# Five units of the first batch alone, the second batch behind the weights, and float32 turns on TensorE

## The chip, the cores and the metric

The kernel runs on one core of a Trainium2 chip, in one launch. The metric is the device time of a run in microseconds; the kernel before takes 768.63 us (median of 3 runs, 768.42 to 770.69).

Names of engines: PE is TensorE (matmuls and transposes), PEld its weight loads, DVE is VectorE, ACT is ScalarE, POOL is GpSimd, SP is SyncE, whose queue issues nearly all transfers between HBM (the device memory) and SBUF (the on-chip memory). PSUM is the memory that PE writes to.

## The reference

Block-sparse attention followed by a feed-forward layer, cut to what matters:

```python
# q, k, v: 4 batches x 8 heads x 768 positions x 64, float32; blocks of 32 positions (24 blocks)
scores = q @ k.T / sqrt(64)            # masked: a block sees itself and its two neighbours,
                                       # blocks 0 and 23, and 3 sampled blocks; blocks 0 and 23 see all
attn = exp(scores - max); attn /= attn.sum(-1, keepdims=True) + 1e-9
x = (attn @ v).transpose(0, 2, 1, 3).reshape(3072, 512)
h = x @ w_in                           # 512 x 2048, float64 in HBM
g = np.where(h > 0, h, exp(min(h, 0)) - 1)
out = g @ w_out                        # 2048 x 512, float64 in HBM; out is float32
```

## The kernel before

The 3072 rows are worked off in 24 units of 128 rows (four query blocks of 32). The four batches are taken as two pairs; batch 0 of a pair is x=0 and batch 1 is x=1. A unit of `of_one` (L608) takes four neighbouring blocks of one batch, a unit of `of_two` (L605) two blocks of both batches, and the special unit blocks 0 and 23 of both. `ALONE` (L303) says how many units of the first pair are of one batch: 1, so unit 0 is of x=0, unit 1 of x=1, and all later ones need both batches.

**Precision.** A float32 value is carried as two float16 parts, a high and a low one (the high part is a cast, the low one the value less the high part), and products are taken over the parts. Queries and keys are split and turned (transposed), values are split with a column of ones beside them.

**Attention of a unit** (`attention`, L656), by pairs of heads (four pairs hp=0..3): PE makes the scores (L786, 32 matmuls of 32 columns for one pair: against `kG`, where POOL has gathered the sampled blocks' keys, L748 and L755, and against the neighbours in `kT`); DVE takes the maxima (L797); ACT the exponentials `e` (L815); then `e` is cast to the high part of `p` (L818) and the low part taken from it (L820, DVE or POOL); `p` (eight squares of 128) is turned by `turn16` (L374), either on PE into PSUM with a copy out by ACT or DVE (L391), or by a transfer on SP's queue (L377); PE multiplies with the values (L835, 64 matmuls); DVE adds the two parts (L844). After four pairs DVE normalizes (L852 to L854), `x` is split (L863, L864) and turned into `xT` (L866). The values lie in HBM as `vd`, written by the kernel in float16 with the ends of the sequence doubled (L569), and a unit's rows are fetched into the rooms `VT` by SP (L726 to L728) and by an indirect transfer on POOL (L733).

**Feed-forward** (`ffn`, L870), for two units at once (U=0..11), in 8 steps f2 of two chunks of 128 of the 2048 hidden values: layer 1 (L883, 24 matmuls into `h`), the activation on ACT and DVE (L893, L895, L891), its split into `g` (L898, L900), layer 2 (L906, 12 matmuls into the two `o`).

**Weights.** 32 pieces of 512 KB, float64. Each is loaded as pairs of integers into a room that waits to be filled (`wo_room`, the place of later output weights, or `st4`), and made into float16 parts by six operations (`weights`, L417): ACT scales the upper words (L439), ACT or DVE shifts (L444, L448), DVE takes signs (L451) and joins (L455), ACT or DVE casts the high part (L459), DVE or POOL takes the low part (L462). A step f2 of the feed-forward needs four pieces.

**What sets the order.** All operations are given to a planner (`Plan`, L43) with a priority, the engines that may take them with a cost each, what they read and write, and the buffer they need (`rooms`, L260, says how many there are of each tag). `Plan.order` (L70) places them in one list, engine by engine, and the engines then work off their lists in that order, waiting on semaphores. So the numbers at the end (L921 to L951) decide what stands ahead of what on each engine, SP's queue included. There: the keys and values of x=0 at -500, those of x=1 at `SECOND` = -110, the weights from `WI` = -100 on, `WID` = 3 apart, the feed-forward U at `F0 + T * U` with steps `F2` = 4.5 apart, attention `LEAD` = 130 ahead of it. Units below `NPE` = 4 have all their turns on PE; units 4 to 13 have the first two pairs (`PP` = 2) turned on PE and the rest by transfers.

Lines touched: `turn16` (L374), `weights` with its rooms (L401 to L472), `zero_rows` (L480), `keys` and `values` (L576, L586), the copy into `kG` (L738 to L757), `e32`, `p` and `pT` (L810 to L823), `norm` and the split of `x` (L850 to L867), `ffn` (L870) and the numbers (L303, L921 to L951).

## Time and profile before

| | |
|---|---|
| device time, median of 3 runs | 768.63 us |
| profiled execution (its span; nothing outside the span is recorded) | 780.8 us |
| PE busy | 703.2 us, 90% of the span |
| DVE, ACT, POOL busy | 504.7, 406.1, 398.8 us |
| bytes moved by transfers | 126.34 MB, 162 GB/s over the span |

The profile is of one execution, 12.2 us (1.6%) longer than the median of the timed runs; durations come from it. Busy time says that an engine had an instruction under way. The granted clock tells how fast PE ran: 1.0 is 2.4 GHz and 0.5 is 1.2 GHz. Lines (L883) are those of the listing above.

### The profile page before, as it was taken

Reading aid. Unit: us, or ns where it says so; the run is one execution under the profiler, and the core shown is the slowest. Engines: PE = TensorE matmul, PEld = TensorE weight load, DVE = VectorE, ACT = ScalarE, POOL = GpSimd, SP = SyncE. Lnnn points to the kernel's source line nnn. Section 1 sums busy time; section 2 is a strip of 40 time slices with the busy share of each in tenths; the row PEclk is TensorE's granted clock in tenths of the full one; section 3 lists DMA queues with packets and bytes.
Section 4 is the critical chain, followed back from the end, with each engine's and each line's share of the span. In section 5 each row is a group of like instructions: output and inputs, shape, how many; then the busy total and the mean of one; then the engine's idle time right before and its main releaser. Section 6 shows DMA issues by size and latency. Waiting matters only on the chain.

```text
span 780.8 us, 26302 instructions
## 1 busy us (share of the span) xinstructions
PE 703.2 (90%) x11064; PEld 476.2 (61%) x11064; DVE 504.7 (65%) x849; ACT 406.1 (52%) x723; POOL 398.8 (51%) x605
## 2 busy tenths in 40 slices
PE   6445466999999998999999999999999999999997
PEld 3334355666665765666866766657656667676663
DVE  7788778898866772767677665757555546644121
ACT  4597767897753743535575443425414344342221
POOL 2588567677553345554375454645625337443121
PEclk7555569999999999999999999999999999999999
DMA  9899998889749697769947987987349459652101
GB/s 240 263 275 288 261 257 209 215 158 208 154 91 264 187 192 164 161 133 203 221 87 142 171 149 150 183 144 166 76 94 229 69 103 216 141 97 45 38 1 27
DMA packets 217006, 126.34 MB, mean 162 GB/s; under 512 B 173944, under 2 KB 194552, under 8 KB 216888
## 3 DMA queue, kind: packets, MB, share of 16 engines
q1 hardware_dynamic: 211608, 107.09, 64.8%
q0 software_dynamic: 5280, 17.58, 8.9%
q8 instruction: 86, 1.41, 0.8%
q14 instruction: 32, 0.26, 0.1%
HBM read 82.05 MB, written 13.21 MB: 122 GB/s over the span
## 4 chain that ended last, share of the span: by engine, by line
PE 80%; issue 4%; DMA 4%; DVE 4%; ACT 3%; POOL 3%; POOLq 1%; SPq 1%; another core or an unknown queue 1%; ACTq 0%; DVEq 0%
PE o L906 32%; PE h L883 31%; PE s L786 6%; PE w L835 4%; PE av L835 2%; PE s L385 2%; DMA wo<-in_moe_w_out_dram 2%; ACT e L815 1%; PE av L385 1%; POOLq L751 1%; DMA VT<-vd 1%; POOL kG L755 1%; DMA raw<-in_sampled_blocks_dram 1%; POOL kG L748 1%
## 5 line engine op out<-in xcount | busy, mean ns | idle before, releaser
L883 PE MATMUL h<-xT,wi 128*128 128x256 f16 x2304 | 281.6, 275 | 4.7 <-DVE fe L891 4.0
L906 PE MATMUL o<-wo,g 128*128 128x512 f16 x1152 | 274.9, 381 | 0.9 <-issue 0.6
L883 PEld LDWEIGHTS <-wi 128*128 128x128 f16 x2304 | 220.0, 98 | 53.8 <-issue 7.1
L906 PEld LDWEIGHTS <-g 128*128 128x128 f16 x1152 | 107.0, 98 | 111.2 <-issue 4.2
L900 POOL TENSOR_TENSOR g<-fe,g 128x512 f16<-128x512 f32 x75 | 90.0, 1200 | 150.8 <-DVE g L299 134.8
L820 POOL TENSOR_TENSOR p<-e,p 128x512 f16<-128x512 f32 x94 | 113.1, 1206 | 93.8 <-DVE p L299 46.4
L893 ACT ACTIVATE fe<-h 128x512 f32<-128x512 f32 x96 | 57.3, 596 | 178.0 <-PE h L883 165.1
L891 DVE SCALAR_TENSOR_TENSOR fe<-h,fe 128x512 f32<-128x512 f32 x96 | 66.0, 688 | 92.9 <-ACT fe L895 84.4
L815 ACT ACTIVATE e<-s,m 128x256 f32<-128x256 f32 x208 | 86.2, 470 | 74.7 <-POOL p L820 37.1
L755 POOL COPY kG<-kT 128x128 int32 x264 | 78.5, 341 | 44.9 <-PE s L786 25.9
L797 DVE TENSOR_REDUCE m<-s 128x2 f32<-128x512 f32 x104 | 70.1, 686 | 44.4 <-PE s L786 41.4
L733 POOL DMA_INDIRECT VT<-vd,idx x66 | 64.5, 977 | 25.1 <-issue 10.1
L895 ACT ACTIVATE fe<-fe,gs 128x512 f32<-128x512 f32 x96 | 69.4, 723 | 2.4
L844 DVE TENSOR_REDUCE x<-w 128x130 f32<-128x260 f32 x64 | 27.2, 426 | 59.7 <-PE w L835 56.9
L835 PEld LDWEIGHTS <-pT 128*32 128x32 f16 x3456 | 43.2, 97 | 36.1 <-issue 33.7
L786 PE MATMUL s<-kG,qT 128*32 128x160 f16 x704 | 44.8, 247 | 9.6 <-ACT e L815 7.0
L786 PEld LDWEIGHTS <-qT 128*32 128x32 f16 x1664 | 33.2, 99 | 31.8 <-issue 26.7
L786 PE MATMUL s<-kT,qT 128*32 128x96 f16 (+1 forms) x832 | 48.5, 225 | 1.2 <-issue 1.0
L786 PE MATMUL s<-kT,qS 128*32 128x96 f16 (+1 forms) x832 | 48.3, 225 | 0.5 <-issue 0.5
L786 PE MATMUL s<-kG,qS 128*32 128x160 f16 x704 | 44.2, 246 | 4.1 <-DVE qS L299 2.7
L299 DVE CAST p<-e 128x512 f16<-128x512 f32 x59 | 32.0, 546 | 13.3 <-DMA pT<-p 6.1
L786 PEld LDWEIGHTS <-qS 128*32 128x32 f16 x1664 | 34.5, 102 | 6.0 <-DVE qS L299 3.0
(134 smaller groups left out, 812.5 us busy)
## 6 DMA issues: line engine op xcount, KB each, us to landing
VT<-vd SPq DMA_DIRECT2D x44, 195.0 KB
VT<-vd SPq DMA_DIRECT2D x22, 390.0 KB
wo<-in_moe_w_out_dram SPq DMA_DIRECT2D x12, 512.0 KB
st<-in_q_dram SPq DMA_DIRECT2D x40, 128.0 KB
out_dram<-ro SPq DMA_DIRECT2D x38, 128.0 KB
wo<-in_moe_w_in_dram SPq DMA_DIRECT2D x9, 512.0 KB
st<-in_moe_w_in_dram SPq DMA_DIRECT2D x7, 512.0 KB
VT<-vd SPq DMA_DIRECT2D x12, 260.0 KB
```

What stands on the lines that cost most here:

```text
L733: nc.gpsimd.indirect_dma_start(VT[0:96, 2 * vt.slot, xs[0] : xs[-1] + 1].rearrange("p b x -> p (b x)"), None, d.ap, bass.IndirectOffsetOnA ...
L755: nc.gpsimd.tensor_copy(dst[:, :, r * 16 : (r + 1) * 16], src[:, :, bass.ds(at[r], 16)])
L786: nc.tensor.matmul(dst, lhsT=qq.ap[:, h, j * BLK : (j + 1) * BLK], rhs=mv, start=first, stop=(y == 1 and qq is qS and o0 + w == 256))
L797: nc.vector.tensor_reduce(m.ap[:, 2 * c : 2 * c + 2] if sp else m.ap[:, 6:8], ss[c].ap, axis=AX.X, op=ALU.max, negate=True)
L815: nc.scalar.activation(e32.ap[:, y, :], ss[c].ap[:, y, :], AF.Exp, bias=m.ap[:, 6 + y : 7 + y])
L820: plan.add(LO, t + PITCH * hp + 1, margin=MO, fn=lambda e, e32=e32, p=p: ENG[e].tensor_tensor(p.ap[:, 1, :], flat(e32.ap), p.ap[:, 0, :], ...
L835: nc.tensor.matmul(av.ap[j * BLK : (j + 1) * BLK, y, v0:], lhsT=pts[c].ap[:, pl * 4 + y * 2 + z, j * BLK : (j + 1) * BLK], rhs=VT[:, room, ...
L883: nc.tensor.matmul(h.ap[:, a, :], lhsT=w[:, wl, cs], rhs=x.ap[:, xl, cc, :], start=(n == 0), stop=(n == 3 * NCC - 1))
L891: nc.vector.scalar_tensor_tensor(e32.ap, h.ap, -IH * GS, e32.ap, op0=ALU.mult, op1=ALU.min)
L895: plan.add({"ACT": 0.68}, p0 + 2.6, lambda e, e32=e32: nc.scalar.activation(e32.ap, e32.ap, AF.Relu, bias=gs_col, scale=-GS), r=[e32], w=[ ...
L900: plan.add(LO, p0 + 2.6, margin=MO, fn=lambda e, e32=e32, g=g: ENG[e].tensor_tensor(g.ap[:, 1], e32.ap, g.ap[:, 0], op=ALU.subtract), r=[e ...
L906: nc.tensor.matmul(o.ap, lhsT=g.ap[:, gl, f % 2, m * P : (m + 1) * P], rhs=wo[f][:, wl, :], start=(f == 0 and n == 0), stop=(f == NFC - 1 ...
```

## The change

The first pair's first five units are now of x=0 alone (`ALONE` = 5), then five of x=1, then the special unit and one of both batches; before, all but two needed both. Only the keys and values of x=0 are loaded ahead of the weights, values first. Those of x=1 follow at `SECOND` = 28, behind most of the weights, by the functions `keys` and `values` that the second pair has used so far. Until then the room of x=1's keys, `kT1`, is lent to the weights as three more landing rooms. Feed-forward 0 stands at -50 with steps 12 apart, feed-forward 1 at 60.

A new function `turn32` turns float32 squares on PE (four of 128 x 128 in place of eight in float16) into PSUM; ACT casts the high part out of PSUM, and DVE takes the low part as PSUM less the high part. It replaces the cast, the low part and the `turn16` of `p` and `x` where these went by PE: all pairs and `x` of units 0 to 5 (`NPE` = 6, was 4), the first two pairs of units 6 to 13 without the special one. From unit 6 on, `e` and `p` of the odd pairs lie together in one `st4` buffer (not close to the change of pairs).

The diff, cut:

```diff
+class Part:
+    def __init__(self, whole, view):
+        self.whole, self.view = whole, view
+    @property
+    def ap(self):
+        return self.view()
...
-    ALONE, SPECIAL, SECOND = 1, 8, -110.0
-    MO, MC, ML, MH = -0.6, 0.0, 0.5, 0.6
+    ALONE, SPECIAL, SECOND, KT_LAST, ST_FIRST = 5, 10, 28.0, 32, 20
+    MO, MC, ML, MH, MW = -0.6, 0.0, 0.5, 0.6, 0.0
...
+    def turn32(t, src, part, high, low, new=(), w=(), name="", bank="s"):
+        pt = buf(bank, [P, 4, P], F32, ps)
+        def go(e):
+            for i in range(4):
+                nc.tensor.transpose(pt.ap[:, i, :], part(i), ident)
+        plan.add({"PE": TURN32}, t, go, r=[src], new=[pt], code=8, name=name + "p")
+        plan.add(HIGH, t, lambda e: scaled(e, high(), pt.ap), r=[pt], new=new, w=w, margin=MC, port=False, name=name)
+        plan.add({"DVE": 0.69}, t, lambda e: nc.vector.tensor_tensor(low(), pt.ap, high(), op=ALU.subtract),
+                 r=[pt, *new, *w], w=[*new, *w], port=False, name=name + "l")
+
+    TURN32, HIGH = 0.6, {"ACT": 0.6}
...
-    used = {j: j - 20 for j in range(NFC // 2)}
+    kt_room = [fixed(flat(kT[1])[:, 2048 * j : 2048 * (j + 1)].bitcast(I32).rearrange("p (e w) -> p e w", w=2))
+               for j in range(3)]
+    ROOMS = {**{j: wo_room[j] for j in range(NFC // 2)}, **{-3 - j: r for j, r in enumerate(kt_room)}}
+    used = {j: j - 20 for j in ROOMS}
...
-        free_rooms = [j for j in used if j > n // 4]
-        if n // 4 >= 4:
+        free_rooms = [j for j in used if j > n // 4 or j < -2 and n < KT_LAST]
+        if n >= ST_FIRST:
...
-        plan.add({"SP": 0.5}, prio, load, new=[s] * tagged, w=[s] * (not tagged), dma=1.9, name=f"wl{i}")
+        plan.add({"SP": 0.5}, EARLY_AT if n < EARLY else prio, load, new=[s] * tagged, w=[s] * (not tagged), dma=1.9, name=f"wl{i}")
...
-        plan.add(SHIFT, prio, lower, margin=MH, r=[s], new=[low3], name=f"ws{i}")
+        plan.add(SHIFT, prio, lower, margin=MW, port=False, r=[s], new=[low3], name=f"ws{i}")
...
-        plan.add({"ACT": 0.6, "DVE": 0.43}, prio, high, margin=MH, r=[s], w=[hi_done, *over], name=f"wh{i}")
+        plan.add({"ACT": 0.6, "DVE": 0.43}, prio, high, margin=MW, r=[s], w=[hi_done, *over], name=f"wh{i}")
...
-    def keys(g, x, c, prio, via="DMA"):
+    def keys(g, x, c, prio, via="DMA", over=()):
...
-        turn16(prio, n, lambda: kT[x][:, :, c * P : (c + 1) * P], via, w=[kT_buf[x][c]],
+        turn16(prio, n, lambda: kT[x][:, :, c * P : (c + 1) * P], via, w=[kT_buf[x][c], *over],
...
-    def values(g, c, prio):
-        n = buf("st4", [P, 2, H, VW], F16)
+    def values(g, c, prio, xs=(0, 1)):
+        n = buf("st4", [P, len(xs), H, VW], F16)
...
-                e32, p, pT = buf("e", [P, 2, 256], F32), buf("p", [P, 2, 512], F16), buf("g" if u == 1 else "pT", [P, 8, P], F16)
+                pT = buf("g" if u == 1 else "pT", [P, 8, P], F16)
+                if u >= WIDE and hp % 2 and not sp and not NUP - OFF <= u < NUP + ON:
+                    both = buf("st4", [P, 2, 512], F32)
+                    e32 = Part(both, lambda both=both: both.ap[:, 0].rearrange("p (y k) -> p y k", y=2))
+                    p = Part(both, lambda both=both: both.ap[:, 1].bitcast(F16).rearrange("p (l k) -> p l k", l=2))
+                else:
+                    e32, p = buf("e", [P, 2, 256], F32), buf("p", [P, 2, 512], F16)
...
+                if hp < via[1] and not sp:
+                    turn32(t + PITCH * hp + TURN, eb, lambda i, e32=e32: flat(e32.ap)[:, i * P : (i + 1) * P],
+                           lambda pT=pT: pT.ap[:, 0:4], lambda pT=pT: pT.ap[:, 4:8], new=[pT], name=f"pt{u}.{hp}", bank=bank)
+                    continue
...
+        if via[2] == "PE":
+            turn32(t + PITCH * 3 + TIMES + 3, xf, lambda i: xf.ap[:, i * P : (i + 1) * P],
+                   lambda: xt.ap[:, 0, :, ts_], lambda: xt.ap[:, 1, :, ts_],
+                   new=new, w=[] if new else [xt], name=f"xt{u}", bank="av")
+            return
...
-    EVEN, NEXT = 6, 14.0
+    EVEN, NEXT = 6, 4.0
+    WIDE, OFF, ON = 6, 3, -1
...
-    TWO, AHEAD, T, F0, LEAD, NPE = 6, 16.0, 58.0, 60.0, 130.0, 4
-    WI, WID, F2, LAG = -100.0, 3.0, 4.5, 14.0
-    V1, K1 = 70.0, 16.0
+    TWO, AHEAD, T, F0, LEAD, NPE = 6, 16.0, 58.0, 60.0, 130.0, 6
+    WI, WID, F2, LAG = -66.0, 3.0, 4.5, 14.0
+    V1, K1, SV = 70.0, 16.0, 8.0
+    EARLY, EARLY_AT = 5, -95.0
...
-    for x in range(2):
-        p = -500 if x == 0 else SECOND
-        places = [wo_place(j) for j in range(6)] if x == 0 else [wi_place(j) for j in range(2, 8)]
...
+    F1, F2X = (-50.0, 60.0), 12.0
...
+            if u == 4 * ALONE // 4:
+                for c in range(NKC):
+                    keys(0, 1, c, SECOND + 2 * c, "PE", kt_room)
+                for c in range(NKC):
+                    values(0, c, SECOND + SV + 2 * c, (1,))
...
-        ffn(U, t)
+        ffn(U, F1[U] if U < len(F1) else t, F2X if U == 0 else F2)
```

How this moves instructions, at three places. **SP's queue where the weights begin**, before (L511 loads keys and values, `wi<-in_k_dram` being the keys of x=1; L569 writes values to `vd`; L429 loads a weight piece):

```order
L511 DMA wo<-in_v_dram 128x8x128 x3
L511 DMA wi<-in_k_dram 128x8x128 x3
L569 DMA vd_175<-st_171 16x1040 x2
L569 DMA vd_175<-st_171 7x16x1040 x2
L429 DMA wo<-in_moe_w_in_dram 128x4x256
L640 DMA st_428<-in_q_dram 128x8x64
```

and now the same queue at the last weight pieces (L457 and L461 load pieces, L605 keys and L618 values of x=1, `kT_71` is the room of x=1's keys):

```order
L457 DMA kT_71<-in_moe_w_in_dram 128x4x256
L605 DMA st_2644<-in_k_dram 128x8x64
L461 DMA kT_71<-in_moe_w_out_dram 128x1024
L605 DMA st_2657<-in_k_dram 128x8x64
L461 DMA kT_71<-in_moe_w_out_dram 128x1024
L605 DMA st_3109<-in_k_dram 128x8x64
L618 DMA st_3132<-in_v_dram 128x8x64
L605 DMA st_3151<-in_k_dram 128x8x64
```

The keys of x=1 stood ahead of all weights and now stand between and behind the last of them, the values behind all.

**PE where feed-forward 0 begins**, before (L786 are scores, of unit 3 here; `h<-xT,wi` is layer 1):

```order
L786 LDWEIGHTS qS_2075
L786 MATMUL s_2130<-kT_71,qS_2075 32x96
L786 LDWEIGHTS qS_2075
L786 MATMUL s_2130<-kT_71,qS_2075 32x96
L883 LDWEIGHTS wi
L883 MATMUL h_2164<-xT_1553,wi 128x256
```

and now (L880 multiplies unit 1's last pair with the values, L412 is a float32 turn, of unit 1's `x`):

```order
L880 MATMUL av_1542<-VT,g_1397 32x65
L880 LDWEIGHTS g_1397
L880 MATMUL av_1542<-VT,g_1397 32x65
L412 MATMUL av_1589<-ident,xn_1581 128x128 x4
L936 LDWEIGHTS wi
L936 MATMUL h_1607<-xT_1488,wi 128x256
```

Before, 416 score matmuls (three units and a quarter) and 12 turns of keys stood ahead of the first layer 1; now it comes as soon as unit 1 is turned, with 256 score matmuls and 6 turns of keys ahead.

**DVE over unit 0's pairs**, before (L797 maxima, L299 a cast, L451 and L455 weights):

```order
L797 TENSOR_REDUCE m_750<-s_713 128x2
L299 CAST p_790<-e_752 128x512
L797 TENSOR_REDUCE m_805<-s_757 128x2
L451 SCALAR_TENSOR_TENSOR w_792<-wo,w_792 128x512
L455 SCALAR_TENSOR_TENSOR wo<-wo,w_792 128x512
```

and now (L831 maxima, L415 the low part of a float32 turn, L528 the low part of a query, L479 and L483 weights):

```order
L831 TENSOR_REDUCE m_687<-s_641 128x2
L415 TENSOR_TENSOR pT_679<-o_632,pT_679 128x512
L528 SCALAR_TENSOR_TENSOR n_691<-st_431,n_691 128x8x64
L415 TENSOR_TENSOR pT_727<-o_674,pT_727 128x512
L831 TENSOR_REDUCE m_806<-s_693 128x2
L479 SCALAR_TENSOR_TENSOR w_638<-kT_71,w_638 128x512
```

Each turned pair has one low part on DVE, read from PSUM, where it had casts, low parts and copies shared out over three engines.

## Rows read from the trace of the kernel before

**Rows 1.** The page's 40 slices of 19.5 us: granted clock of PE in tenths.

```profile
PEclk7555569999999999999999999999999999999999
```

**Rows 2.** Six stretches: length, busy PE, PEld, DVE, ACT, POOL (instructions), clock, DMA, GB/s.

```profile
0.00:50.70 50.70, 26.48 (x327) 18.78 (x328) 37.63 (x73) 31.53 (x49) 25.26 (x69) 0.65 0.92 263
50.70:124.90 74.20, 43.98 (x964) 33.53 (x962) 60.53 (x91) 57.91 (x101) 52.01 (x80) 0.62 0.98 264
124.90:196.20 71.30, 63.20 (x1134) 43.62 (x1134) 61.44 (x97) 57.64 (x104) 51.00 (x84) 0.95 0.85 189
196.20:302.00 105.80, 103.64 (x1715) 68.67 (x1714) 76.01 (x130) 57.54 (x106) 47.38 (x63) 1.00 0.80 174
302.00:370.00 68.00, 62.13 (x1081) 42.16 (x1079) 42.73 (x76) 31.80 (x56) 36.63 (x43) 0.97 0.85 170
370.00:780.80 410.80, 403.76 (x5852) 269.42 (x5849) 226.40 (x386) 169.64 (x312) 186.49 (x270) 1.00 0.63 122
```

**Rows 3.** PE in order of time: start, length, line, operation, idle before.

```profile
34.79 0.33 PE L786 MATMUL s<-kG,qT 128*32 128x160 f16 x4
...
113.00 1.97 PE L883 MATMUL h<-xT,wi 128*128 128x256 f16 x12
```

**Rows 4.** The weights' last load and last low part: durations, then first and last start.

```profile
L433 SPq DMA_DIRECT2D st<-in_moe_w_out_dram x4: 346/360/364, 115.0 to 179.5; - x4
...
L462 POOL TENSOR_TENSOR wo<-st,wo x2: 1170/1296/1422, 185.1 to 195.1; 128x512 f16<-128x512 f32 x2
```

**Rows 5.** Groups of DVE, shapes apart: count, busy us, mean ns, idle before.

```profile
L797 DVE TENSOR_REDUCE m<-s 128x2 f32<-128x512 f32 x104 | 70.1, 686 | 44.4 <-PE s L786 41.4 <-remote 2.5
L891 DVE SCALAR_TENSOR_TENSOR fe<-h,fe 128x512 f32<-128x512 f32 x96 | 66.0, 688 | 92.9 <-ACT fe L895 84.4 <-POOL kG L755 3.1 <-ACT kT L297 1.8
...
L299 DVE CAST p<-e 128x512 f16<-128x512 f32 x59 | 32.0, 546 | 13.3 <-DMA pT<-p 6.1 <-ACT e L815 5.0 <-issue 1.0
L671 DVE COPY qS<-qT 64x1024 f16<-64x1024 f16 x40 | 30.8, 771 | 1.0
...
L820 DVE TENSOR_TENSOR p<-e,p 128x512 f16<-128x512 f32 x18 | 16.4, 911 | 0.2
...
L844 DVE TENSOR_REDUCE x<-av 128x130 f32<-128x260 f32 x32 | 13.5, 422 | 19.2 <-remote 10.9 <-PE av L835 7.7 <-PE s L385 0.6
...
L497 DVE SCALAR_TENSOR_TENSOR VT<-wi,VT 128x512 f16<-128x512 f32 x6 | 8.5, 1415 | 0.0
...
L497 DVE SCALAR_TENSOR_TENSOR fe<-wi,fe 128x512 f16<-128x512 f32 x6 | 4.3, 741 | 0.0
```

**Rows 6.** From 196.2 us on, one line each: L883, L906, L786, L835, L385 (busy, matmuls).

```profile
196.20:780.80 584.60, 247.65 (x2040) 1.00 0.69 137
196.20:780.80 584.60, 254.01 (x1068) 1.00 0.69 137
196.20:780.80 584.60, 51.69 (x2432) 1.00 0.69 137
196.20:780.80 584.60, 47.21 (x2848) 1.00 0.69 137
196.20:780.80 584.60, 19.27 (x256) 1.00 0.69 137
```

**Rows 7.** The chain that ended last: start, length, what.

```profile
299.20 0.56 PE s L786 x32
299.76 2.70 PE o L906 x12
302.46 1.31 PE h L883 x12
303.77 0.46 PE av L835 x32
```

**Rows 8.** PE in order of time: a float16 turn of eight squares, and what follows it.

```profile
310.81 0.61 PE L385 MATMUL av<-ident,p 128*128 128x128 f16 x8 [3.29 <-issue]
311.35 0.25 PE L786 MATMUL s<-kG,qT 128*32 128x160 f16 x4
```

More of the change, by code (lines that the diff above doesn't have):

```diff
@@ L315 @@
     kG = const([P, rooms["kG"], 2, H, KW], F16, "kG")
-    ident = sb.tile([P, P], F32, tag="x32", bufs=rooms["x32"], name="ident")
+    ident = const([P, P], F32, "ident")
     nc.gpsimd.memset(ident, 1.0)
@@ L377, in turn16 @@
             plan.add({"SP": 1.3}, t, lambda e: nc.sync.dma_start_transpose(dst(), flat(src.ap)),
-                     r=[src], new=new, w=w, dma=2.4, name=name)
+                     r=[getattr(src, "whole", src)], new=new, w=w, dma=2.4, name=name)
             return
+        got = getattr(src, "whole", src)
         pt = buf(bank, [P, 8, P], F16, ps)
@@ L420, in weights @@
         w = (wi if i < NFC else wo)[f]
[L421 removed]
+        s = ROOMS[stage[n]] if stage[n] in ROOMS else buf("st4", [P, DM, 2], I32)
         over = [wo_room[f // 2]] if i >= NFC else []
@@ L478, with zero_rows, put @@
     vd += [[(buf("vd1", [ROWS, 2 * RW], F16, dr), (0, 1))] for _ in range(1, NPAIR)]
-    def zero_rows(prio):
-        z = buf("st4", [P, 2 * RW], F16)
+    def zero_rows(prio, later):
+        z = buf("x32", [P, RW], F16)
         plan.add({"POOL": 0.6}, prio, lambda e: nc.gpsimd.memset(z.ap[0:BLK, :], 0.0), new=[z], name="zero")
         for g in range(NPAIR):
-            for n in (0, NB - 1):
-                for d, xs in vd[g]:
-                    def put(e, d=d, xs=xs, n=n):
-                        nc.sync.dma_start(d.ap[n * BLK : (n + 1) * BLK, :], z.ap[0:BLK, 0 : RW * len(xs)])
-                    plan.add({"SP": 0.45}, prio, put, r=[z], new=[d] if n == 0 else [],
-                             w=[d] if n else [], dma=0.3, name=f"z{g}")
+            for d, xs in vd[g]:
+                for n in (0, NB - 1):
+                    for i in range(len(xs)):
+                        def put(e, d=d, n=n, i=i):
+                            nc.sync.dma_start(
+                                d.ap[n * BLK : (n + 1) * BLK, i * RW : (i + 1) * RW], z.ap[0:BLK, :])
+                        first = n == 0 and i == 0
+                        plan.add({"SP": 0.45}, prio if xs == (0,) else later, put, r=[z], new=[d] if first else [],
+                                 w=[] if first else [d], dma=0.3, name=f"z{g}")
     def split(prio, s, n, high, low, scale, new, name="", src=None):
@@ L756, in copy @@
                                 dst[:, :, r * 16 : (r + 1) * 16], src[:, :, bass.ds(at[r], 16)])
-                plan.add({"POOL": 1.75 if two else 2.5}, t - 6, copy, r=keys_in, new=[kg], name=f"kg{u}")
+                plan.add({"POOL": (1.5 if two else 2.1) + (1.1 if fresh() else 0.0)}, t - 6, copy, r=keys_in, new=[kg], name=f"kg{u}")
         x32 = buf("x32", [P, H, D + 1], F32)
@@ L853, in norm @@
             nc.vector.reciprocal(total, total)
-            nc.vector.tensor_tensor(x, x, total.unsqueeze(2).to_broadcast([P, H, D]), op=ALU.mult)
-        plan.add({"DVE": 0.95}, t + PITCH * 3 + TIMES + 1.5, norm, r=[x32], w=[x32], name=f"nx{u}")
+            nc.vector.tensor_tensor(
+                x if xf is None else by_head(xf.ap), x, total.unsqueeze(2).to_broadcast([P, H, D]), op=ALU.mult)
+        plan.add({"DVE": 0.95}, t + PITCH * 3 + TIMES + 1.5, norm, r=[x32], w=[x32], new=[xf] if xf else [], name=f"nx{u}")
         U, a = u // 2, u % 2
```

41 lines of the change are left out of this document (22 added, 19 removed).

## The prediction

> **What bounds the kernel now.** I read the slices of the page first: PE's granted clock is at its lower level, 1.2 GHz, for most of the first six slices and at 2.4 GHz from then on [rows 1]. So there are two stages. The stretches say where they part [rows 2]. From 196.2 us to the end PE is busy for 103.6 + 62.1 + 403.8 = 569.5 of 584.6 us at nearly full clock: that stage is bound by PE's own work, and no faster other engine shortens it. In the first 124.9 us PE is busy 70.5 us, mostly at half clock, while transfers take 92 to 98% of their engines and DVE 74 to 82% of the time. That is the start. It ends when the weights are ready: the last piece is issued at 179.5 us, and its low part ends at 196.2 us [rows 4]. Meanwhile the first scores come at 34.8 us and the first layer 1 only at 113.0 us [rows 3].
>
> So the time is T1, when the last weight part is done, plus the PE work that is then left. Before: 196.2 + 584.6 = 780.8 us, the span of the profiled execution. It lies 12.2 us above the median of the timed runs, 768.63; I work in the profile's time and multiply by 768.63 / 780.8 = 0.984 at the end.
>
> **T1 in the changed kernel.** DVE is the busiest of the three helpers in each of the first three stretches [rows 2], all weight pieces pass it, and its list is in fixed order. Up to T1 it was busy 37.6 + 60.5 + 61.4 = 159.6 us. I count what the new order puts ahead of the last low part.
>
> Gone from there, since units 4 to 6 and the second batch now stand behind: 12 maxima (28 to 16) at 0.686, 6 joins at 0.422, low parts of x=1's keys and values, 6 at 0.741 and 6 at 1.415, and 6 halves of turned queries at 0.771 us [rows 5]: 8.2 + 2.5 + 4.4 + 8.5 + 4.6 = 28.2 us. 16 low parts of p, x, g and weights at 0.911: 14.6. Eight casts of p and x at 0.546: 4.4. Seven copies and three activations out of PSUM at L891's 0.688: 6.9. A norm and three query parts, estimated from these rows: 4. Together 58.1 us.
>
> Added: 19 low parts of float32 turns, which no row shows; they read 128x512 out of PSUM as L891 does, 0.688 us [rows 5] (between a cast's 0.546 and L820's 0.911, so 10.4 to 17.3 us): 13.1. 17 more casts at 0.546, 16 of them of weights, which the planner may now give to DVE without a margin: 9.3. Six shifts at about 0.69: 4.1. Together 26.5 us. So DVE has 159.6 - 58.1 + 26.5 = 128.0 us of work ahead of T1.
>
> To the fourth piece's low part (before at 50.7 us) the order gives DVE as much as before, 37.6 us; 90.4 us remain. DVE was busy 60.53 / 74.2 = 82% of the second stretch and 86% of the third [rows 2]. If it never waited, T1 would be 50.7 + 90.4 = 141 us; at 82%, 161 us. I take the third stretch's 86%, because transfers were not full there (0.85 against 0.98): 50.7 + 90.4 / 0.862 = 156 us.
>
> Transfers don't set this. By GB/s and lengths [rows 2] before had moved 13.3 + 19.6 + 10.3 = 43.2 MB when the last piece was issued. Ahead of that issue the new order lacks 11 MB of it (two key chunks and all values of x=1, their copies in `vd`, the value rooms and queries of three units, the query transfers), so about 32 MB; at the first stretches' 263 GB/s the last piece would go out at 123 us and, with the 16.7 us that before had from there to the end, T1 would be 139 us.
>
> **PE work left at T1.** The other engines' order tells what PE has behind that point. Before [rows 6]: 2040 matmuls of layer 1, 1068 of layer 2, 2432 score matmuls, 2848 with the values, 256 float16 squares. Now: 2112, 1074, 2816, 3072, some 200 float16 squares, and 100 float32 squares. So the start no longer works ahead on units 4 to 6: more attention is left, although T1 is earlier. By durations [rows 7, 8], 1.31 / 12 for layer 1, 2.70 / 12 for layer 2, 0.56 for 32 scores, 0.46 for 64 with the values (the chain's x32 counts half of them), 0.54 for eight float16 squares (310.81 to 311.35): 72 x 0.109 + 6 x 0.225 + 12 x 0.56 + 3.5 x 0.46 - 7 x 0.54 = 7.9 + 1.4 + 6.7 + 1.6 - 3.8 = 13.8 us more.
>
> The 25 float32 turns of four squares are not in any row. At best a square costs what a float16 one does, 0.27 us a turn; at worst it takes four passes of 128 columns, as much as a layer-2 matmul of 512, 4 x 0.225 = 0.90 us. A float32 turn of four squares moves the bytes of a float16 turn of eight, so I take the nearest row's 0.54 us: 13.5 us, range 6.8 to 22.5.
>
> A float16 turn shows 0.54 / 8 = 68 ns for a square with its weight load [rows 8]. The Trainium skill (TensorE: Matmul & The Clock Gate, Weight-path perf modes) says that fast weight load is off for float32, and its section on LDWEIGHTS gives such a load as columns over 1.2 GHz, 107 ns for 128 as an estimate; that speaks against the change. By it a turn is at least 0.43 us and the 25 cost 10.7 us or more; by the row, 13.5. No run here shows a float32 load.
>
> Left: 584.6 + 13.8 + 13.5 = 612 us, so a span of 156 + 612 = 768 us.
>
> **What costs nothing.** The 19 float32 turns ahead of T1 lie in PE's idle time (54.4 us of the first 124.9 [rows 2]); if that cover were gone, they cost 19 x 0.54 = 10 us. The joint buffers of e and p from unit 6 on can only take away waits of ACT and DVE; PE's whole idle time after 196.2 us is 15.1 us, spread over 584.6, and I credit 2 us of it, none if those waits were others. Moving the last keys and values behind the weights puts 12 loads, 7 writes and the rooms of unit 5 behind them on SP's queue; they are hidden as long as feed-forward 0's end, unit 4 and feed-forward 1 keep PE busy (next part). POOL's second read of its index registers for a unit of one batch is covered by POOL's idle time (20 to 26 us in each of the first three stretches [rows 2]); uncovered it would delay scores, which the next part prices.
>
> Sum: 768 - 2 = 766 us, against 780.8: 14.8 us or 1.9% less. In timed runs 766 x 0.984 = 754 us.
>
> **Rivals.** (a) *The start goes at the speed of transfers.* DVE waited before mostly because data and freed rooms came late; with 11 MB less and three more landing rooms it need not. Then T1 is 139 to 141 us and the span 751 us, 739 timed. For it: 98% transfers in the second stretch. Against: the third stretch had transfers at 85% and DVE still waited 14% [rows 2].
>
> (b) *Half of the gain is lost on PE.* Float32 turns take four passes: 0.36 us more on each of 25, 9 us; the span is 775 us, 763 timed. The trace has no float32 matmul that would deny it. The same time comes out if DVE stays at 82% (T1 161) and the joint buffers give nothing.
>
> The granted clock is at half for the slices in which PE does little but turns and scores [rows 1]. [...]
>
> (c) *Slower: the second batch comes too late.* Its keys can be written only when the last weight has left `kT1`, and its values go by SP's queue, a split, HBM and back. Between T1 and unit 5's first matmul with values PE has in order 15 groups of layer 1, 66 layer-2 matmuls, 7 score sets, two value sets, 7 float16 and 8 float32 turns: 19.7 + 14.9 + 3.9 + 0.9 + 3.8 + 4.3 = 47 us by rows 7 and 8. A chain longer than that is paid in full. Before took 34.8 us from the first instruction to unit 0's first scores with a like chain [rows 3]. It must reach 47 + 15 + 2.3 = 64 us to eat the gain and pass the 0.3%; at 68 us the span is 787, 775 timed. Against: 34.8 us is far from 64, and the first key loads of x=1 are issued ahead of the last weights.
>
> (d) *No change:* the attention that is pushed back returns in full as PE waits in the next 100 us; DVE was at 76.0 / 105.8 = 72% there [rows 2] and would get some 30 us more. 768.6 us.
>
> **How the numbers follow.** Chances: forecast 0.48 (754 timed), (a) 0.22 (739), (b) 0.16 (763), (c) 0.09 (775), (d) 0.05. A measurement of this kernel can tell about 0.3% (2.3 us) from no change. Faster: forecast, (a) and (b), 0.86, less 0.01 for the top of (b). Same: (d) and that 0.01, 0.06. Slower: (c), 0.09. The forecast's own range: T1 150 to 161 and turns 0.27 to 0.90 us give spans of 753 to 780, 742 to 768 timed. The range to hold 8 in 10 takes in most of (a) and all of (b): 737 to 768 us.
>
> **What would show it.** Right: the first layer 1 near 80 us instead of 113; the last weight's low part at 150 to 161 us; in the stretch up to it DVE at 86% and PE at full clock earlier; from then on PE busy over 97% for some 610 us. A float32 square's matmul start to start tells the turn: 0.54 us for four, or 0.27, or 0.9. (a) would show as a last low part at 140 us and DVE over 95%. (c) would show as PE idle behind `kG<-kT` or `VT<-vd` of unit 5. The prediction is wrong if T1 is not earlier than 180 us, or if PE waits for more than 25 us after it.

## The result, and the profile after

The changed kernel takes 762.31 us (median of 12 runs, 758.0 to 768.3) against 769.68 us (12 runs, 766.8 to 772.0) for the kernel before on the same chip: a ratio of 0.9898, 95% interval 0.9879 to 0.9917. That is 7.4 us less where the forecast had 14.6 us less (754). The sign was right, the time lies in the range, and the size was half of what I said. An execution now and then falls into a slower state; ratios and profiles here leave such executions out, and so `after_again` has no profile in the table below.

The profiled execution has a span of 758.5 us and was timed at 760.2. The granted clock by slices (here of 19 us) is the row that answers to [rows 1]:

```profile
PEclk8585899999999999999999999999999999999999
```

It is near full speed in the fifth slice and at full speed from the sixth on, where before that was the seventh. The stretches, with the columns of [rows 2], cut at the same kinds of places:

```profile
0.00:48.00 48.00, 27.11 (x364) 17.77 (x364) 32.69 (x68) 26.07 (x44) 20.35 (x62) 0.71 0.81 229
48.00:81.30 33.30, 17.44 (x368) 12.88 (x367) 24.71 (x47) 15.33 (x29) 18.72 (x30) 0.60 1.08 293
81.30:154.20 72.90, 58.72 (x888) 39.53 (x887) 63.39 (x109) 55.98 (x100) 40.79 (x54) 0.95 0.66 179
154.20:260.00 105.80, 104.41 (x1949) 73.23 (x1948) 79.25 (x137) 65.43 (x124) 61.91 (x135) 1.00 0.84 180
260.00:328.00 68.00, 68.00 (x1136) 46.31 (x1135) 49.25 (x85) 39.62 (x73) 28.75 (x34) 1.00 0.94 210
328.00:758.50 430.50, 422.17 (x6293) 281.41 (x6286) 221.07 (x400) 191.03 (x349) 198.32 (x280) 1.00 0.69 131
```

Up to 154.2 us DVE was busy 32.69 + 24.71 + 63.39 = 120.8 us, and from there on PE 594.6 of 604.3 us. PE in order of time, the first scores and the first layer 1, as in [rows 3]:

```profile
32.76 0.33 PE L820 MATMUL s<-kG,qT 128*32 128x160 f16 x4 [2.51 <-ACT qT L308]
...
74.82 0.37 PE L936 MATMUL h<-xT,wi 128*128 128x256 f16 x1 [0.69 <-ACT xT L308]
```

The first layer 1 stands at 74.8 us, before at 113.0. The weights' last load and last low part, as in [rows 4]:

```profile
L461 SPq DMA_DIRECT2D kT<-in_moe_w_out_dram x8: 346/347/2043, 24.7 to 137.2; - x8
...
L490 POOL TENSOR_TENSOR wo<-kT,wo x5: 1165/1173/1387, 85.1 to 153.0; 128x512 f16<-128x512 f32 x5
```

So T1 is 153.0 + 1.17 = 154.2 us (forecast 156, before 196.2). What PE did behind it, one line each, as in [rows 6]: layer 1 (L936), layer 2 (L959), scores (L820), values (L880), float16 squares (L397), float32 squares (L412):

```profile
154.20:758.50 604.30, 254.55 (x2112) 1.00 0.75 148
154.20:758.50 604.30, 254.40 (x1073) 1.00 0.75 148
154.20:758.50 604.30, 57.40 (x2816) 1.00 0.75 148
154.20:758.50 604.30, 50.92 (x3072) 1.00 0.75 148
154.20:758.50 604.30, 13.25 (x184) 1.00 0.75 148
154.20:758.50 604.30, 15.12 (x96) 1.00 0.75 148
```

The sum of the last two against [rows 6]: 28.4 us of turns where 19.3 were. PE in order of time, float32 turns of four squares and what follows them, beside the float16 turn of [rows 8]:

```profile
101.66 0.60 PE L412 MATMUL s<-ident,e 128*128 128x128 f32 x4
102.09 0.38 PE L936 MATMUL h<-xT,wi 128*128 128x256 f16 x2
...
404.48 0.66 PE L412 MATMUL av<-ident,st 128*128 128x128 f32 x4
405.07 0.25 PE L820 MATMUL s<-kG,qT 128*32 128x160 f16 x4
```

From the first square to the next kind of work a turn takes 0.43 to 0.59 us here. Over the 22 single turns behind T1 it is 0.44 to 0.62, 0.53 in the middle; I had taken 0.54.

### The profile page after: what moved, and what is told of

The parts are those of the page before. It is cut to its first block, busy times and chain, and to the rows that moved or that the text cites. A ratio compares the mean times of both kernels' runs of the same rounds, so it can differ in the third digit from the quotient of the medians.

```text
span 758.5 us, 26215 instructions
## 1 busy us (share of the span) xinstructions
PE 697.9 (92%) x10984; PEld 471.1 (62%) x10984; DVE 470.4 (62%) x843; ACT 393.5 (52%) x715; POOL 368.8 (49%) x591
## 4 chain that ended last, share of the span: by engine, by line
PE 79%; DVE 6%; DMA 4%; issue 3%; ACT 3%; SPq 2%; POOL 1%; POOLq 0%; ACTq 0%; DVEq 0%
PE h L936 32%; PE o L959 31%; PE s L820 6%; PE w L880 4%; PE av L880 2%; PE s L397 2%; DMA st<-in_q_dram 1%; DMA wo<-in_moe_w_in_dram 1%; DMA VT<-vd 1%; DVE w L479 1%; PE av L412 1%; DMA wo<-in_k_dram 1%; POOL wi L490 1%; POOL VT L763 1%; DVE m L831 1%
## 5 line engine op out<-in xcount | busy, mean ns | idle before, releaser
L936 PE MATMUL h<-xT,wi 128*128 128x256 f16 x2304 | 282.7, 276 | 7.7 <-POOL wi L490 4.9
L959 PE MATMUL o<-wo,g 128*128 128x512 f16 x1152 | 273.2, 380 | 1.0 <-DVE g L953 1.0
L936 PEld LDWEIGHTS <-wi 128*128 128x128 f16 x2304 | 220.4, 99 | 56.5 <-POOL wi L490 6.2
L953 POOL TENSOR_TENSOR g<-fe,g 128x512 f16<-128x512 f32 x83 | 99.6, 1201 | 171.3 <-DVE g L310 123.1
L959 PEld LDWEIGHTS <-g 128*128 128x128 f16 x1152 | 107.0, 98 | 111.4 <-DVE g L953 1.5
L946 ACT ACTIVATE fe<-h 128x512 f32<-128x512 f32 x96 | 57.3, 597 | 163.7 <-PE h L936 156.6
L831 DVE TENSOR_REDUCE m<-s 128x2 f32<-128x512 f32 x104 | 69.7, 685 | 35.9 <-PE s L820 35.4
L856 ACT ACTIVATE e<-s,m 128x256 f32<-128x256 f32 x148 | 61.4, 470 | 49.2 <-DVE m L831 35.0
L865 POOL TENSOR_TENSOR p<-e,p 128x512 f16<-128x512 f32 x37 | 44.9, 1217 | 61.5 <-ACT p L308 19.0
L880 PEld LDWEIGHTS <-pT 128*32 128x32 f16 x3456 | 42.4, 97 | 32.4 <-issue 27.8
L820 PE MATMUL s<-kG,qT 128*32 128x160 f16 x704 | 43.5, 242 | 8.1 <-ACT e L856 3.8
L820 PEld LDWEIGHTS <-qT 128*32 128x32 f16 x1664 | 32.0, 98 | 29.4 <-issue 22.3
L820 PE MATMUL s<-kT,qT 128*32 128x96 f16 (+1 forms) x832 | 47.0, 221 | 0.2 <-ACT e L856 0.2
L820 PE MATMUL s<-kT,qS 128*32 128x96 f16 (+1 forms) x832 | 47.0, 221 | 0.0
L528 DVE SCALAR_TENSOR_TENSOR n<-st,n 128x512 f16<-128x512 f32 x42 | 34.2, 818 | 15.0 <-ACT n L308 14.8
L820 PE MATMUL s<-kG,qS 128*32 128x160 f16 x704 | 42.8, 240 | 0.5 <-issue 0.4
L880 PE MATMUL w<-VT,pT 128*32 128x130 f16 (+1 forms) x2048 | 34.2, 208 | 0.6 <-DVE x L889 0.6
```

Of the source, the lines that this page charges most:

```text
L820: nc.tensor.matmul(dst, lhsT=qq.ap[:, h, j * BLK : (j + 1) * BLK], rhs=mv, start=first, stop=(y == 1 and qq is qS and o0 + w == 256))
L831: nc.vector.tensor_reduce(m.ap[:, 2 * c : 2 * c + 2] if sp else m.ap[:, 6:8], ss[c].ap, axis=AX.X, op=ALU.max, negate=True)
L856: nc.scalar.activation(e32.ap[:, y, :], ss[c].ap[:, y, :], AF.Exp, bias=m.ap[:, 6 + y : 7 + y])
L880: nc.tensor.matmul(av.ap[j * BLK : (j + 1) * BLK, y, v0:], lhsT=pts[c].ap[:, pl * 4 + y * 2 + z, j * BLK : (j + 1) * BLK], rhs=VT[:, room, ...
L936: nc.tensor.matmul(h.ap[:, a, :], lhsT=w[:, wl, cs], rhs=x.ap[:, xl, cc, :], start=(n == 0), stop=(n == 3 * NCC - 1))
L946: plan.add({"ACT": 0.57}, p0 + 2.6, lambda e, h=h, e32=e32: nc.scalar.activation(e32.ap, h.ap, AF.Exp, scale=IH), r=[h], new=[e32], name=f ...
```

## The experiments

Twelve runs in three sets, each set on one chip and each timed beside the kernel before. The three chips differ: the kernel before took 769.67 us in the first set (as beside the changed kernel above, 769.68, which I therefore count to the first chip), 784.89 in the second, 782.72 in the third. So ratios are to be compared, and times only within a set; a ratio, too, can differ from chip to chip, as `after_again` shows. For each: T1, PE's busy and idle time behind it (of the profiled execution, by stretches cut at T1), its span, and the ratio to the kernel before.

| set, kernel | T1 | PE busy behind T1 | PE idle behind T1 | span | ratio (95%) |
|---|---|---|---|---|---|
| before, the profile of the forecast | 196.2 | 569.5 | 15.1 | 780.8 | |
| 1 before_again | 195.2 | 564.6 | 8.8 | 768.6 | 1.0001 (0.9985 to 1.0016) |
| changed kernel (result above) | 154.2 | 594.6 | 9.7 | 758.5 | 0.9898 (0.9879 to 0.9917) |
| 1 no_joint: order + turns | 153.9 | 596.1 | 17.8 | 767.8 | 0.9998 (0.9978 to 1.0018) |
| 1 order_alone: order + joint rooms | 157.3 | 595.2 | 14.9 | 767.3 | 1.0008 (0.9983 to 1.0034) |
| 1 turn_alone: turns | 180.2 | 581.6 | 17.2 | 779.0 | 1.0101 (1.0056 to 1.0146) |
| 2 joint_alone: joint rooms | 196.3 | 570.5 | 19.0 | 785.7 | 1.0079 (1.0050 to 1.0108) |
| 2 joint_turn: turns + joint rooms | 185.1 | 580.2 | 18.4 | 783.7 | 1.0003 (0.9978 to 1.0029) |
| 2 dve_load | 168.2 | 601.8 | 24.3 | 794.3 | 1.0128 (1.0101 to 1.0154) |
| 2 dma_load | 156.6 | 597.9 | 25.0 | 779.5 | 0.9971 (0.9944 to 0.9997) |
| 3 after_again: changed kernel | | | | | 0.9981 (0.9950 to 1.0012) |
| 3 wide8 | 154.0 | 597.6 | 19.7 | 771.3 | 0.9927 (0.9899 to 0.9955) |
| 3 wide_all | 157.5 | 599.4 | 23.8 | 780.6 | 0.9988 (0.9961 to 1.0016) |
| 3 order_only: order | 162.7 | 612.8 | 37.5 | 813.0 | 1.0426 (1.0402 to 1.0451) |

In each of these profiles 4.8 to 5.8 us of the idle time lie behind PE's last matmul, while the last outputs leave; only the rest are waits within the work: 10.1 us in the profile of the forecast, 3.8 in `before_again`, 4.3 in the changed kernel, 12.2 in `no_joint`.

### Where the 12 us of the first profile were

No edit: the kernel before once more.

> The kernel before, unchanged, profiled anew. The changed kernel's timed runs lie 1.7 us above their spans, so a median of 769.7 us means a usual span of about 768; the profile on which the forecast was built had 780.8. Theory: that execution lost some 12 us in its start by chance; the new profile has its last low part of a weight near 184 us (not 196.2), PE work left of about 584, span 768. Rival 1: the start is the same, 196 us, and the 12 us were in the stretch from 302 to 370 us (an instruction-fetch stall of 3.3 us at 307.5 and half clock from 312 to 315 us): then T1 is 196 and what is left 572. Rival 2: the loss is spread, every stage 1.6% shorter (T1 193, left 575). Timed against the kernel before: the same within 0.3%.

Measured: 768.6 us. The weights' last low part in it, and the two stretches cut at it:

```profile
L462 POOL TENSOR_TENSOR wo<-st,wo x2: 1156/1158/1160, 184.0 to 194.0; 128x512 f16<-128x512 f32 x2
```

```profile
0.00:195.20 195.20, 135.08 (x2431) 98.00 (x2432) 163.83 (x261) 148.32 (x254) 126.16 (x231) 0.72 0.93 238
195.20:768.60 573.40, 564.63 (x8635) 378.06 (x8633) 345.02 (x589) 257.28 (x470) 270.56 (x375) 1.00 0.72 139
```

T1 is the same, 195.2 us; what PE had left took 573.4 and not 584.6 us. My theory (the start) fell, and rival 1 holds: 11.2 of the 12.2 us sat behind T1, 6.3 of them as idle and 4.9 as longer busy time. In the profile of the forecast PE stood 3.29 us ahead of the float16 turn at 310.81 with nothing that it waited for [rows 8]; here that wait is absent. In the second set, joint_alone, whose order is that of the kernel before up to unit 8, shows it again (PE in order of time):

```profile
306.39 1.48 PE L902 MATMUL h<-xT,wi 128*128 128x256 f16 x12
311.17 0.61 PE L397 MATMUL av<-ident,p 128*128 128x128 f16 x8 [3.30 <-issue]
```

So the wait can come back at the same place, and is not mere chance of one execution. The forecast's profile (780.8) fits the second and third sets' chips, the times that it was scaled to (768.6) the first's; that it was taken on such a chip is an inference from this wait and its span. The chip is not the whole cause either: `turn_alone`, on the first chip, has 9.3 us of waits of this kind. The name in the expectation, a stall of instruction fetch ("for code" in that of `joint_turn`), is not shown: a 16 KB transfer of the instruction queue ends at 306.4 us, 1.1 us ahead of the wait, but the same transfer ends at 302.0 us in `before_again`, where PE goes on at once.

### The three parts, alone and in pairs

order_alone leaves the order and the joint rooms and turns float16:

```diff
-                if hp < via[1] and not sp:
+                if False and hp < via[1] and not sp:
...
-        xf = buf("xn", [P, DM], F32) if via[2] == "PE" else None
+        xf = None
```

> The changed kernel with its new order, rooms and joint buffers, but p and x turned as float16 everywhere, as before. Theory (the order carries the gain): the median stays at least 4 us below the kernel before, 762 to 766 us; DVE gets 19 low parts of 0.91 us in place of 19 of about 0.7 and more casts ahead of the last weight part, so that part ends at 155 to 165 us, and a float16 turn costs PE 0.54 us where a float32 one costs 0.44, so the work left is within 2 us of the changed kernel's 604. Rival (the float32 turns carry it): 768 to 770 us, T1 at 175 or later.

Measured: no gain, 1.0008. T1 was as the theory had it (157.3), and so was the work left (595.2). What was not expected is that PE waits 14.9 us behind T1, and that its clock is at half in part of it (0.83 on average in the stretch from 220 to 240 us). The order's 38 us are spent, but the rival is no better: its T1 of 175 us or later did not come, and the turns alone (below) bring nothing.

no_joint takes away the joint rooms:

```diff
-    WIDE, OFF, ON = 6, 3, -1
+    WIDE, OFF, ON = 99, 3, -1
```

> The changed kernel without the joint buffers of e and p (each has its own room all through, as before). Theory: PE hardly waits after 154 us, so they are worth nothing: within 0.3% of the changed kernel (760 to 765 us) and the same start. Rival: they carry some of the gain, 2 to 4 us: 765 to 767 us, with idle time of PE behind p or e between 160 and 740 us.

Measured: 769.51 us, ratio 0.9998; the theory is refuted and the rival was too low. The start is the same (T1 153.9), PE's work too (596.1 against 594.6); 8.1 of the 9.3 us between the spans are idle time of PE behind T1. The edit does more than take rooms away: the planner places everything anew, and from 194 us on PE's order is another one. PE's longest waits behind T1, line, what for, us in total, times, longest:

```profile
PE h L936 <- DVE fe L944: 2.6, 1, 2.6
PE s L820 <- ACT e L856: 1.8, 2, 1.3
PE w L880 <- DMA pT<-p: 1.6, 1, 1.6
PE s L820 <- DVE qS L701: 1.5, 1, 1.5
PE h L936 <- DMA xT<-xn: 1.4, 2, 1.2
PE s L820 <- POOL kG L789: 1.4, 2, 1.2
PE w L880 <- DVE x L889: 1.3, 1, 1.3
```

and in the same view of the changed kernel:

```profile
PE w L820 <- ACT e L856: 1.7, 1, 1.7
PE s L397 <- DVE n L528: 0.6, 1, 0.6
PE w L880 <- DVE x L889: 0.6, 1, 0.6
PE s L820 <- POOL kG L789: 0.5, 1, 0.5
```

The helpers are late, each a little. ACT itself waits for want of a room: the same view for ACT's exponentials, first without the joint rooms, then with them.

```profile
ACT e L856 <- POOL p L865: 63.6, 29, 4.4
```

```profile
ACT e L856 <- POOL p L865: 9.3, 5, 3.8
```

Here ACT waits for the low part that frees a room of `e`: 63.6 us behind T1 without joint rooms, 9.3 with them. That this is what makes PE wait is not shown. With joint rooms ACT waits longer for the maxima (L831), 44.6 us against 11.4; the kernel before has 44.5 us of such waits of ACT for a room, and PE waits only 3.8 us within its work; and PE's own waits for the exponentials are 1.8 us without joint rooms and 1.9 with them. What grows without them are PE's waits for the activation (`fe`), the turns by transfer, the queries and `kG`.

turn_alone puts `turn32`, as in the change, into the kernel before, for all units and pairs that are turned on PE there (not only the first four units, of which the expectation speaks), and gives the identity a room of its own:

```diff
+                if hp < via[1] and not sp:
+                    turn32(t + PITCH * hp + TURN, e32, lambda i, e32=e32: flat(e32.ap)[:, i * P : (i + 1) * P],
...
+                    continue
...
+        if via[2] == "PE":
+            turn32(t + PITCH * 3 + TIMES + 3, xf, lambda i: xf.ap[:, i * P : (i + 1) * P],
```

> The kernel before with its own order and its own list of units, only p and x of its first four units turned as float32. Theory: a small part of the gain: DVE and POOL are spared casts and low parts in the start, but the weights still stand behind the second batch; T1 3 to 8 us earlier than the kernel before, median 766 to 770 us. Rival (the turns carry the gain): 761 to 764 us. Rival (float32 turns cost more than they free): 771 us or more.

Measured: 1.0101, slower; by its number the second rival holds. T1 came 15 us earlier (180.2), more than I expected, but 17 us more work was left behind it, and PE waited 17.2 us there, 9.3 us of it with nothing that the profile shows (4.5 us at once at 218 to 223 us).

joint_alone puts only the joint rooms into the kernel before (there from unit 8 on, the first one behind all its weights); joint_turn adds the same lines to turn_alone:

```diff
+    WIDE, OFF, ON = 8, 3, -1
...
+                if u >= WIDE and hp % 2 and not sp and not NUP - OFF <= u < NUP + ON:
+                    both = buf("st4", [P, 2, 512], F32)
```

> The kernel before with its order and its float16 turns, and the joint rooms of e and p alone, from unit 8 on (the first unit behind all weights there). Theory (the joint rooms pay only in the new order): the profiled executions of the kernel before wait 8.8 us on PE behind T1, of which 3 us behind ACT's exponentials; so 0 to 3 us, 767 to 770 us timed. Rival (the joint rooms are the whole gain, whatever the order): the changed kernel without them was at 769.5 us and with them at 762.3, so they bring 7 us here as well: 761 to 764 us, and order and turns together bring nothing.

> The kernel before with float32 turns and joint rooms of e and p (from unit 8 on), in its own order: the changed kernel without its order. Theory: float32 turns alone made it 779 us, with T1 at 180 us and waits on PE for code and half clock behind T1; joint rooms take away 0 to 7 us of that: 772 to 779 us, so the order is worth 10 us or more once the other two are there. Rival (the order is worth nothing, turns and joint rooms make the gain): 760 to 765 us.

Measured: joint_alone 1.0079, slower, which neither theory had; joint_turn 1.0003. Against the changed kernel's 0.9898 on the first chip the order is then worth about 1%, as the theory said; against dma_load on joint_turn's own chip (below; the changed kernel with transfers added that nothing reads, 0.9971) it is 0.3%, and the intervals overlap. So the worth of the order is not settled. The order alone is order_alone with one line more:

```diff
-    WIDE, OFF, ON = 6, 3, -1
+    WIDE, OFF, ON = 99, 3, -1
```

> The changed kernel's order alone: p and x turned as float16, e and p in rooms of their own all through. Theory (time is T1 plus PE's work left plus PE's waits): T1 near 157 us as with the joint rooms, PE busy 595 us behind it, 12 to 22 us of waits: ratio 0.996 to 1.010. Rival (the order is worth its 40 us of T1 less 30 us of attention pushed back, whatever else is there): 0.985 to 0.990.

Measured: 1.0426, far outside. PE waits 37.5 us behind T1, is busy for 612.8 us where I expected 595, and its clock dips; its slices of 20 us, and its longest waits behind T1:

```profile
PEclk8576798899898999999999996999999999999999
```

```profile
PE s L820 <- issue: 9.3, 18, 1.1
PE s L820 <- ACT e L856: 8.3, 5, 3.2
PE h L936 <- DVE fe L944: 3.3, 3, 1.7
PE w L880 <- DMA pT<-p: 2.1, 2, 1.2
```

So no single part is faster (1.0101, 1.0079, 1.0426), no pair is (0.9998, 1.0008, 1.0003), and all three together are 1% faster on one chip. On the first chip alone the parts do not add up: float32 turns cost 1.0% when put into the kernel before, and bring 1.1% when put into order_alone. The other three of these runs are from the other chips, where the whole brings 0.2% (after_again) or 0.3% (dma_load). A reading that fits is that turns and joint rooms pay only where the attention that the order pushes behind T1 would else make the helpers late; it is argued, not shown.

### What paces the start

dve_load issues the sign step of each weight twice; dma_load adds a transfer of 256 KB behind each weight load. In dma_load PE, DVE and ACT work off the same operations in the same order as in the changed kernel, so it also stands in for that kernel on the second chip:

```diff
         def sign(e):
-            nc.vector.scalar_tensor_tensor(
+            for _ in range(2):
+                nc.vector.scalar_tensor_tensor(
```

```diff
         def load(e):
...
+            nc.sync.dma_start(
+                spare_dram.ap[n * P : (n + 1) * P, :], w_out.bitcast(I32)[f * P : (f + 1) * P, 0:DM])
```

> The changed kernel with the sign step of every weight piece issued twice on DVE (the second changes no value): 32 more DVE instructions of about 0.7 us, 22 us, all ahead of the last weight's low part, nothing else moved. Theory (T1 is paced by DVE's list, and the time is T1 plus PE's work left): DVE was busy 87% of the stretch from 81 to 154 us, so T1 moves from 154 to 172 to 180 us and the median by as much less what PE can still use: 777 to 788 us. Rival (transfers pace the start, DVE has 22% idle time in it): T1 at 154 to 160 us, 762 to 767 us. Rival (T1 moves but PE's order has other work there): T1 at 175, median below 772 us.

> The changed kernel with one more transfer behind each weight load on SP's queue: 256 KB from HBM to HBM, never read, 32 of them, 8.4 MB, all ahead of T1. Transfers took 79% of their engines up to T1 there, and moved 219 GB/s, so 8.4 MB are about 32 to 38 us of all engines. Theory (DVE paces the start): only the stretch from 48 to 81 us, where transfers are full, is stretched, T1 moves by 4 to 12 us and the median to 765 to 774 us. Rival (transfers pace the start): T1 moves by 30 us or more, 785 us or more. Rival (transfers are hidden altogether): within 0.3% of the changed kernel.

Measured, first dve_load, then dma_load up to T1 (columns as in [rows 2]):

```profile
0.00:168.20 168.20, 108.20 (x1606) 73.38 (x1606) 141.91 (x253) 97.25 (x169) 79.62 (x145) 0.74 0.70 201
```

```profile
84.00:156.60 72.60, 61.03 (x894) 41.66 (x893) 64.10 (x110) 56.29 (x100) 40.61 (x54) 0.93 0.83 250
```

The 8.4 MB cost nothing that can be seen: T1 156.6 us, ratio 0.9971, where the changed kernel had 0.9981 in the third set. Transfers were at 250 GB/s in a stretch where the changed kernel moved 179. Rival (a) is out, by its own price; my own 4 to 12 us for T1 were too many. In dve_load the 32 extra steps are 22 us of DVE. Against dma_load, on the same chip, DVE had 19.3 us more to do up to T1 (141.9 for 122.6), T1 came 11.6 us later and the median 11.4 us (794.82 against 783.43): the time follows T1 about one for one, but only some 60% of DVE's extra work reaches T1. DVE's waits up to T1 fell from 34.0 to 26.3 us, and that took up the rest. My figure of 18 to 26 us was too high.

### The gain on another chip, and other counts of joint rooms

after_again is the changed kernel unchanged; wide8 has joint rooms from unit 8 on, wide_all in the units about the second pair's first too (the two new lines, in this order):

```diff
-    WIDE, OFF, ON = 6, 3, -1
+    WIDE, OFF, ON = 8, 3, -1
...
+    WIDE, OFF, ON = 6, 0, 0
```

> The changed kernel, unchanged, profiled and timed anew beside the three others of this set. The kernel before was 2% slower in the last set than in the first two. Theory: the change's ratio stays (0.988 to 0.992), because T1 and PE's work left hardly depend on that. Rival: behind T1 PE waits more when everything is slower, and the ratio rises to 0.994 or more.

> The changed kernel with joint rooms of e and p from unit 8 on in place of unit 6. Theory (the rooms themselves free ACT and PE, unit by unit): two of the units that have them lose them, so a small part of the 7 us comes back: 0 to 1.5 us over the changed kernel, ratio 0.990 to 0.992. Rival (taking rooms for e and p makes the planner write another order behind T1, and it is that order's waits which differ): the ratio can be anything from 0.988 to 1.005, and is as likely over 0.995 as under it.

> The changed kernel with joint rooms of e and p in the units next to the first units of the second pair of batches too, where they are left out now. Theory (rooms): PE waits 9.7 us in all behind 154 us, 1.7 and 0.2 of it behind ACT's exponentials; the joint rooms compete with the values' rooms there, so no gain to be had: within 0.4% of the changed kernel on either side. Rival (another order): anything from 0.988 to 1.005 of the kernel before.

Measured: the changed kernel's ratio is 0.9981 on this chip (interval 0.9950 to 1.0012), not told from no change, and its median, 783.53 us, is even 0.8 us above that of the kernel before; by its number the rival holds. PE's first 3448 matmuls (of 10984) are the same, in the same order, in the changed kernel, dma_load and wide_all. Their stretch behind T1, on the first, the second and the third chip:

```profile
154.20:254.40 100.20, 99.40 (x1831) 69.83 (x1830) 73.81 (x126) 62.74 (x118) 57.41 (x123) 1.00 0.83 181
156.60:266.20 109.60, 100.50 (x1832) 70.28 (x1830) 72.25 (x127) 62.76 (x118) 57.20 (x124) 1.00 0.75 166
157.50:266.40 108.90, 101.33 (x1831) 70.37 (x1830) 72.57 (x127) 60.66 (x114) 58.22 (x123) 1.00 0.71 169
```

PE waits 0.8 us of it on the first chip, 9.1 on the second and 7.6 on the third. So the same order of PE's work costs 7 to 8 us more there, in the first 100 us behind T1. The kernel before loses less: where joint_alone still has its order (196.3 to 346.6 us), PE waits 6.5 us, and in `before_again` 2.4 us (195.2 to 337.8 us). Over all that lies behind T1, wide_all has 23.8 us of idle time. Its longest waits there:

```profile
PE s L820 <- issue: 4.1, 9, 0.8
PE w L880 <- issue: 2.8, 3, 2.0
PE av L412 <- DVE x L889: 2.6, 1, 2.6
PE s L820 <- DVE qS L701: 1.4, 1, 1.4
```

wide8 has less of the joint rooms and is faster: a median of 776.64 us against 783.53 for the changed kernel and 782.72 for the kernel before, ratio 0.9927. So more joint units did not help here: starting at unit 6, or using all of them, was no better than starting at unit 8. The theory of the rooms unit by unit fell, and the rival fits, since each choice of rooms lets the planner write another order behind T1 (PE's differs from the changed kernel's from 222 us on in wide8, from 254 us in wide_all, on the changed kernel's time). wide8 beats the kernel before on the one chip where it ran; the 0.5 points over the changed kernel are at the edge of the two intervals, which just overlap.

## Why the forecast came out at twice the gain

**T1: right.** 154.2 us for 156, 41.0 us earlier than the re-profile's 195.2 (forecast 40.2). By two errors that cancel: DVE had 120.8 us of work ahead of it and not 128.0, and from 48 us on it was busy 83% (88.1 of 106.2 us) and not 86%. dve_load shows that a list's length over its busy share is too simple: some 40% of what is added goes into waits.

**PE's work left: nearly right.** Against the same profile, busy time rose by 25.1 us (569.5 to 594.6), forecast 27.3. By terms, from the rows above and [rows 6]: layer 1 +6.9 (7.9), layer 2 +0.4 (1.4), scores +5.7 (6.7), values +3.7 (1.6: [rows 6] has 16.6 ns for each of the 224, and I took half of it from the chain), float16 squares -6.0 (-3.8), float32 squares +15.1 (13.5). Against the re-profile it is +30.0, 2.7 more than forecast, since that has less half clock and nine records fewer of layer 1.

**A float32 turn: right, in part by luck.** 0.53 us in the middle; four passes (0.90, rival (b)) are out, and so is a float16 square's price (0.27). The row that I took 0.54 from is not the usual one: of the 24 single float16 turns behind T1 in the same profile 18 took 0.44 to 0.46 us. At the shortest behind T1, 0.44 us, four squares start 109 ns apart. The Trainium skill (TensorE: Matmul & The Clock Gate, LDWEIGHTS) gives a weight load as its columns over 1.2 GHz, from which I had estimated 107 ns for a square and 0.43 us a turn as a floor; this trace agrees with the floor.

**The waits: wrong, and this is the step that failed.** I wrote that the joint buffers can only take away waits, that PE's idle time behind T1 is 15.1 us, "and I credit 2 us of it". That took the waits of before as given, called them spread (5.0 us of them lie behind PE's last matmul and 3.3 in one wait), and asked only what the joint buffers take away. But the new order puts 384 score matmuls and 224 with values more behind T1, with the maxima, exponentials, casts and low parts that go with them, on helpers that have the feed-forward to serve there. Its waits are new ones: PE is idle for 17.8 us without the joint rooms, 14.9 without the turns, 37.5 without both (on another chip), where the kernel before has 8.8 in the first set. With joint rooms and turns it is 9.7. So two errors nearly cancel on the first chip: the new order's waits, which I left out, and the joint rooms, without which the changed kernel loses its whole 7.2 us and which I put at 2.

In numbers, the first chip's profiled executions give -41.0 (T1) + 30.0 (work) + 0.9 (idle) = -10.1 us, where the forecast had -40.2 + 27.3 - 2 = -14.9. The waits account for 2.9 us of the miss, the work for 2.7, and T1 gave back 0.8. The medians are 7.4 us apart, because the changed kernel's profiled execution was 2.1 us below its median and that of the kernel before 0.6 above: another 2.7 us that no step of the forecast stands for. So the waits are the step whose mechanism I had wrong, not the whole of the miss. On the other chips they weigh more: from joint_alone (the nearest to the kernel before that was profiled there) to dma_load or wide_all, idle rises from 19.0 to 24 or 25 us, T1 gains 39 to 40, work costs 27 to 29: some 5 us are left by profiles, and by the timed ratio of the changed kernel 0.2%, not told from nothing.

**The base: lucky.** Multiplying by 0.984 spread the 12 us evenly; they sat behind T1. The product is about the same (768.6 - 14.8 = 753.8), so this didn't cost the forecast its size, but the profile's waits, from which I judged the credit, were not those of the timed executions.

**Rivals.** (a) is refuted by dma_load. (b) gave the right time, 763, for a wrong reason. (c) did not happen: behind T1 PE waits 0.5 us for `kG`, and no wait for `VT` is listed. (d) had the mechanism that matters, attention pushed back that returns as waits of PE, but not its size: in no_joint T1 gains 41.3 us, PE's work takes 31.5 of them and idle time 9.0. On the other chips a good part of the waits comes where (d) put them, in the first 100 us.

Not settled: what makes PE stand with nothing to wait for ("issue": 0.6 us behind T1 in before_again and 9.3 in turn_alone on the first chip, 9.3 in joint_alone on the second); why the same order waits longer on one chip than on another; and whether the joint rooms act by the rooms or by the order that the planner then writes. No run takes the rooms away and keeps the order.

## What to carry to other kernels

Work that is moved out of a start bound by other engines into a stretch bound by PE costs its own time there and also the waits of helpers that were just in time before; price those waits in the new order, not by the old one's idle time. Try the parts of such a change in pairs before dropping one, and on the same chip: here each single part was slower, each pair worth nothing, and the three together 1% faster on the first chip and not told from no change on the third. Take the profile and the times from one chip, and a gain of 1% on more than one.
